# Linear attention and two layers: inputs that come transposed, keys' exponentials on ScalarE, another order, and half the numerators as float32 products

## The chip, the core and the metric

The kernel runs on one core of a Trainium2 chip. The metric is the time on the device, in microseconds (us), of one execution. The engines work through their own instruction streams in order and wait for each other by semaphores: PE multiplies matrices, DVE and ACT work on vectors, POOL does so too, SP issues the transfers. PE's results land in PSUM (eight banks); the other operands lie in SBUF.

## What is computed

Attention with 4 batches of 8 heads, 576 rows, head size 64 and 128 features, and then two layers over 2304 tokens (512 wide, 2048 inner). The weights of the layers come as float64.

```python
def phi(x):
    proj = np.einsum('bhsd,df->bhsf', x, w_phi)
    proj = proj - np.max(np.abs(proj), axis=-1, keepdims=True)
    return np.concatenate([np.exp(proj), np.exp(-proj)], axis=-1)
q_p, k_p = (phi(q), phi(k))
kv = np.einsum('bhsf,bhsd->bhfd', k_p, v)
z = np.sum(k_p, axis=2)
num = np.einsum('bhsf,bhfd->bhsd', q_p, kv)
den = np.einsum('bhsf,bhf->bhs', q_p, z)[..., None] + 1e-06
return (num / den).astype(np.float32)
```

The first layer is `g = h * (1 / (1 + exp(-h)))` with `h = x @ w_in`, the second `g = h * cos(h)`, each followed by `g @ w_out`.

## The kernel before

The 32 heads go in eight sets of four. A product of high accuracy is made of float32r parts: an operand is cast to float32r (hi), the rest is subtracted (lo), and three products hi·hi, hi·lo, lo·hi are added. Products of the keys with the values (kv) are plain float32.

For a set, `load_qk` brings queries and keys as rows; `transpose_in` (L270) turns them on PE into PSUM, ACT casts the result to hi (L284), DVE makes lo (L285). `phi` (L290) makes the projections of one unit (unit 0: the tails of four heads, units 1 to 4: 512 rows of one head each) in a PSUM bank `p`; DVE takes the largest absolute value (L304) and subtracts it (L306). For the keys, `k_exp` lets ACT write both exponentials (L315, L316). For the queries, `q_exp` transposes on PE into the bank `t2` (L324), ACT makes the exponentials (L332), POOL casts them to hi, `qh` (L338), and `q_rest` makes the lower parts `ql` (L346) on DVE or POOL. `kv_parts` sums keys times values (L360 for the tails, L363), cast by ACT (L367), with lo by DVE (L368). `num_parts` makes the numerators and a row of denominators: for each pair of heads (p = 0 or 1) four parts of six products of 288 columns (L389 to L391). `Norm.take` copies them out on ACT (L172); `invert` inverts the denominators on DVE and spreads them by way of two transfers (L186, L189); `apply` multiplies on POOL (L197, L200) into `xy`, the layers' input, which `Inputs.split` parts again (L473, L474).

The order is written by hand. `START` lists the pieces of the first set, `PERIOD` those of one period, in which the queries of a set meet the keys of the next; every piece issues its instructions on all engines at once, so that one list sets the order on each. A name as phi.k.2 is a step, its operand and its unit; a + is one set later, a - one earlier. `piece` is a quarter of the preparation of one weight chunk on ACT, DVE and POOL (L103 to L126). PSUM's banks in the attention: 2 for transposes, 2 for `p`, 1 for `t2`, 3 shared by kv and numerators.

The layers follow (`moe`): h by PE (L509), the functions by ACT, DVE and POOL, y by PE (L558 to L565).

Of the kernel before, what the change touches and what calls it, by code (L numbers as in the profile page):

```python
# [30 lines left out]

MAGIC = 12582912.0
# [16 lines left out]
START = parse("""  # L49
T.k.2 w load.v T.k.0 T.k.1 load.k+ phi.k.0 kx.0 phi.k.1 T.q.0 phi.k.2 phi.k.3 kx.1 T.q.2 kv.0.0.0 kx.2 phi.k.4 kx.3  # L50
kv.0.0.1 phi.q.0 T.k.2+ kx.4 kv.1.0.0 phi.q.1 qx.0 T.q.1 phi.q.2 T.k.0+ kv.1.0.1 qx.1 phi.q.3 ql.1.g T.k.1+ kv.0.1.0
qx.2 phi.q.4 load.k++ ql.2.v kv.1.1.0 qx.3 ql.0.g kv.0.1.1 load.q+ kv.1.1.1 qx.4
# [3 lines left out]
kx.1+ x.2+ num.1.1 x.3+ phi.k.2+ T.k.0++ phi.q.0+ num.1.0 x.4+ load.q++ kx.2+ num.1.2 x.5+ kv.0.0.0+ inv.0 phi.k.0++  # L56
T.k.1++ T.q.2++ num.1.3 x.6+ qx.0+ piece phi.q.1+ ql.0.g+ phi.q.2+ kv.1.0.0+ kv.0.0.1+ piece qx.1+ phi.q.4+ app.0
kv.0.1.0+ qx.2+ ql.1.v+ inv.1 phi.q.3+ kv.0.1.1+ piece qx.4+ kv.1.0.1+ ql.2.v+ kv.1.1.0+ qx.3+ phi.k.3++ T.q.1++
kv.1.1.1+ load.k+++ num.0.0+ kx.0++ ql.3.v+ phi.k.4++ num.0.1+ T.k.2+++ load.v++ num.0.2+ x.0++ kx.3++ kx.4++
phi.k.1++ ql.4.v+ app.1 num.0.3+ x.1++ T.q.0++ piece  # L60
# [3 lines left out]
class Weights:  # L64
    """float64 weights, given as raw words, to float32 parts hi + lo of 12 and 12 bits."""
# [68 lines left out]
class Queue:  # L134
    """Pieces of the weights' conversion, taken one after the other."""
# [23 lines left out]
class Norm:  # L159
    """Numerators over denominators, to x, [dm, token]."""  # L160
# [30 lines left out]
    def apply(self, n, p):  # L191
        nc, xy = self.nc, self.xy
# [7 lines left out]
        nc.gpsimd.tensor_mul(xy[rows, B * NJ + b // 2, c0:c0 + 2, at], t[rows, :, SM:S], r[rows, :, SM:S])  # L200


def attention(tc, q, k, v, w_phi, norm, pieces, then):
    nc = tc.nc
    W = D + 1
    with ExitStack() as ctx:
# [5 lines left out]
        kr, krt, qr, qrt = {}, {}, {}, {}  # L212

        def load_qk(n, src, main, tails, name):
            b, h0 = divmod(n, 2)
            h0 *= 4
            t = fp.tile([P, 4, NJ, D], F32, name=f"{name}r")
            u = fp.tile([P, 2, D], F32, name=f"{name}rt")
            for i in range(2):
                nc.sync.dma_start(u[64 * i:64 * i + 64], src[b, h0 + 2 * i:h0 + 2 * i + 2, SM:S, :].rearrange("h s d -> s h d"))  # L220
            nc.sync.dma_start(t, src[b, h0:h0 + 4, 0:SM, :].rearrange("h (p j) d -> p h j d", j=NJ))
            main[n], tails[n] = t, u
# [33 lines left out]
        # Stationary operands of the last product: columns 0..64 [kv | z] of even heads, 63..127 [z | kv] of odd ones.  # L256
        kvs = [[sp.tile([P, 2, 2, M], F32R, name=f"kv{i}_{part}") for part in ("hi", "lo")] for i, M in enumerate((W, P))]
# [10 lines left out]
        tT = {}  # L268

        def transpose_in(n, name, i):  # L270
            main, tails = (kr, krt) if name == "k" else (qr, qrt)
            N = SM if i < 2 else P
            ps = pp.tile([P, N], F32, name="tp", tag="tp", bufs=2)
            if i < 2:
                for c in range(4):
                    x, jj = divmod(c, 2)
                    src = main[n][:, i + 2 * x, 2 * jj:2 * jj + 2, :].rearrange("p j d -> p (j d)")
                    nc.tensor.transpose(ps[:, c * P:(c + 1) * P], src, ident)
            else:
                nc.tensor.transpose(ps, tails[n].rearrange("p a d -> p (a d)"), ident)  # L280
            sfx = "m" if i < 2 else "t"
            hi = fp.tile([P, N], F32R, name=f"{name}T_hi{sfx}", bufs=2 if i < 2 else 1)
            lo = fp.tile([P, N], F32R, name=f"{name}T_lo{sfx}", bufs=2 if i < 2 else 1)
            nc.scalar.copy(hi, ps)  # L284
            nc.vector.tensor_sub(lo, ps, hi.bitcast(F32))  # L285
            tT[n, name, i] = (hi, lo)
# [3 lines left out]
        def phi(n, name, u):  # L290
            """Unit 0: the tails of the four heads; 1 + 2 p + x: head p + 2 x."""
            i = 2 if u == 0 else (u - 1) // 2
            ns = 1 if u == 0 else 2
            hi, lo = tT[n, name, i]
            ps = pp.tile([P, ns, 2 * F], F32, name="p", tag="p", bufs=2)
            for s in range(ns):
                c = 0 if u == 0 else (((u - 1) % 2) * 2 + s) * P
# [13 lines left out]
        def k_exp(n, u):  # L311
            src = pm.pop((n, "k", u))
# [6 lines left out]
        def q_exp(n, u):  # L319
            src = pm.pop((n, "q", u))  # L320
            ns = 2 if u == 0 else 4
            ps = pp.tile([P, ns, P], F32, name="t2", tag="t2", bufs=1)
            for i in range(ns):
                nc.tensor.transpose(ps[:, i, :], src[:, i, :], ident)  # L324
            if u == 0:
                for p in range(2):
                    qh[n, p] = sp.tile([P, 2, 2, S], F32R, name=f"qh{p}")
                    ql[n, p] = sp.tile([P, 2, 2, S], F32R, name=f"ql{p}")
            p, x = divmod(u - 1, 2)
            for c in range(2):  # L330
                e = sp.tile([P, ns, P], F32, name="et" if u == 0 else "e", bufs=2 if u == 0 else 4)
                nc.scalar.activation(e, ps, AF.Exp, scale=1.0 - 2.0 * c)  # L332
                if u == 0:
                    parts = [(e[:, i, :].rearrange("p (x s) -> p x s", x=2), *(t[n, i][:, c, :, SM:S] for t in (qh, ql))) for i in range(2)]
                else:
                    parts = [(e.rearrange("p a s -> p (a s)"), *(t[n, p][:, c, x, 0:SM] for t in (qh, ql)))]
                for i, (ev, hi, lo) in enumerate(parts):
                    nc.gpsimd.tensor_scalar(hi, ev, 1.0, 0.0, op0=ALU.mult, op1=ALU.add)  # L338
                    rests[n, u, c, i] = (lo, ev, hi)

        def q_rest(n, u, engine):
            """The lower parts of the queries' exponentials."""
            for c in range(2):
                for i in range(2 if u == 0 else 1):
                    lo, ev, hi = rests.pop((n, u, c, i))
                    engine.tensor_sub(lo, ev, hi.bitcast(F32))  # L346
# [3 lines left out]
        def kv_parts(n, p):  # L350
            """18 products of heads p and p + 2: sums over rows of phi(k) with v and ones."""
            out = []

            def mm(c, i):
                def go():
                    if (n, p) not in kvp:
                        kvp[n, p] = pp.tile([P, 2, 2, W], F32, name="kv", tag="kn", bufs=3)
# [7 lines left out]
                    if (c, i) == (1, 8):  # L365
                        hi, lo = (t if p == 0 else t[:, :, :, D - 1:P] for t in kvs[p])
                        nc.scalar.copy(hi, ps)  # L367
                        nc.vector.tensor_sub(lo, ps, hi.bitcast(F32))  # L368
# [334 lines left out]
```

## Time and profile before

| what | us |
|---|---|
| three runs | 1050.23, 1051.86, 1052.01 (median 1051.86) |
| span of the profiled execution, first to last instruction | 1048.8 |
| attention, to the first product of the layers | 228.6 |
| the two layers | 820.2 |

The time of the profiled execution itself is its span of 1048.8 us and what lies around it; the runs shown are 1.4 to 3.2 us above that span. Busy shares of the whole span (PE 97%, DVE 68%, ACT 39%, POOL 35%) are averages over two stages with different limits, so the rows below are taken from the attention by itself.

### The profile page before, as it was taken

What the parts mean: (1) busy time and instruction counts of PE and PEld (TensorE: products, weight loads), DVE (VectorE), ACT (ScalarE), POOL (GpSimd) and SP (SyncE); (2) the same over time, 40 slices, a digit from 0 to 9 for tenths busy, and PEclk for the clock granted to TensorE, in tenths of its full rate; (3) what the DMA queues carried; (4) which work ended last, traced back from release to release, by engine and by line L of the source; (5) the groups of instructions that cost most, each with busy time, mean ns of one, the idle gap of its engine ahead of it and who ended that gap; (6) DMA issues with size and microseconds to landing.
All of it is one profiled execution on the core that took longest, in us unless ns stands there. A gap on an engine that the chain in (4) does not pass through costs nothing.

```text
span 1048.8 us, 15083 instructions
## 1 busy us (share of the span) xinstructions
PE 1019.1 (97%) x6000; PEld 972.5 (93%) x6000; DVE 711.9 (68%) x956; ACT 407.8 (39%) x664; POOL 369.4 (35%) x426
## 2 busy tenths in 40 slices
PE   7999999999999999999999999999999999999998
PEld 7989999989999999999999999899888988998997
DVE  6999999978544344544545567667677867786764
ACT  5655566544433222222223333444333333333332
POOL 3566666656122111201211024334434433343221
PEclk9999999999999999999999999999999999999999
DMA  4544333114111101110110111101110111100112
GB/s 118 139 112 112 99 105 81 47 40 129 41 41 46 55 22 61 41 41 21 61 48 34 41 41 42 40 21 61 41 41 21 61 40 41 27 34 1 61 57 63
DMA packets 62757, 58.33 MB, mean 56 GB/s; under 512 B 30560, under 2 KB 55264, under 8 KB 62688
## 3 DMA queue, kind: packets, MB, share of 16 engines
q1 hardware_dynamic: 62688, 57.38, 18.5%
q8 instruction: 47, 0.77, 0.3%
q14 instruction: 22, 0.18, 0.1%
HBM read 52.49 MB, written 4.79 MB: 55 GB/s over the span
## 4 chain that ended last, share of the span: by engine, by line
PE 61%; DVE 25%; POOL 7%; ACT 4%; issue 1%; DMA 1%; SPq 0%; POOLq 0%; ACTq 0%; DVEq 0%
PE h L509 24%; PE y L558 6%; PE y L560 6%; PE y L559 6%; DVE ql L346 4%; DVE tb L531 3%; DVE tb L530 3%; DVE tb L535 3%; PE kv L363 3%; POOL ta L529 2%; PE y L563 2%; PE y L564 2%; PE y L565 2%; DVE xy L589 2%; POOL gh L536 2%; DVE gl L538 2%
## 5 line engine op out<-in xcount | busy, mean ns | idle before, releaser
L509 PE MATMUL h<-xh,win_hi 128*128 128x384 f32 x768 | 259.1, 337 | 1.7 <-DVE tb L535 1.7
L509 PE MATMUL h<-xl,win_hi 128*128 128x384 f32 x768 | 258.8, 337 | 0.3 <-DVE xl L474 0.3
L509 PE MATMUL h<-xh,win_lo 128*128 128x384 f32 x768 | 258.7, 337 | 0.0
L521 DVE SCALAR_TENSOR_TENSOR ta<-ta,h 128x768 f32<-128x768 f32 x48 | 45.8, 953 | 177.7 <-ACT ta L520 177.7
L509 PEld LDWEIGHTS h<-xh,win_hi 128*128 128x128 f32 x768 | 144.2, 188 | 4.7 <-PE y L565 2.6
L509 PEld LDWEIGHTS h<-xl,win_hi 128*128 128x128 f32 x768 | 144.2, 188 | 2.4 <-DVE xl L474 0.6
L509 PEld LDWEIGHTS h<-xh,win_lo 128*128 128x128 f32 x768 | 144.2, 188 | 0.0
L532 ACT ACTIVATE tb<-tb 128x768 f32<-128x768 f32 x48 | 40.7, 847 | 239.0 <-DVE tb L531 239.0
L558 PE MATMUL y<-gh,wout_hi 128*128 128x384 f32 x384 | 129.5, 337 | 0.2 <-ACT xy L587 0.2
L560 PE MATMUL y<-gh,wout_lo 128*128 128x384 f32 x384 | 129.6, 337 | 0.0
L559 PE MATMUL y<-gl,wout_hi 128*128 128x384 f32 x384 | 129.4, 337 | 0.0
L520 ACT ACTIVATE ta<-h 128x768 f32<-128x768 f32 x48 | 39.0, 813 | 206.4 <-PE h L509 203.1
L563 PE MATMUL y<-wout_hi,gh 128*128 128x512 f32 x288 | 115.0, 399 | 3.3 <-ACT xy L587 1.8
L564 PE MATMUL y<-wout_lo,gh 128*128 128x512 f32 x288 | 114.4, 397 | 0.0
L565 PE MATMUL y<-wout_hi,gl 128*128 128x512 f32 x288 | 114.4, 397 | 0.0
L536 POOL TENSOR_SCALAR gh<-tb 128x768 fp32r<-128x768 f32 x48 | 46.9, 977 | 186.0 <-DVE tb L535 176.0
L538 DVE TENSOR_TENSOR gl<-tb,gh 128x768 fp32r<-128x768 f32 x48 | 75.4, 1570 | 34.3 <-POOL gh L536 34.3
L121 POOL TENSOR_SCALAR wout_hi<-wt 128x512 fp32r<-128x512 f32 x32 | 27.8, 869 | 200.3 <-DVE wt L118 171.1
L121 POOL TENSOR_SCALAR win_hi<-wt 128x512 fp32r<-128x512 f32 x32 | 21.6, 675 | 187.1 <-DVE wt L118 187.1
L589 DVE TENSOR_TENSOR xy<-y,xy 128x384 f32<-128x384 f32 (+1 forms) x126 | 70.8, 606 | 9.7 <-PE y L560 6.0
L535 DVE TENSOR_TENSOR tb<-tb,h 128x768 f32<-128x768 f32 x48 | 45.6, 951 | 46.7 <-ACT tb L533 46.2
L558 PEld LDWEIGHTS y<-gh,wout_hi 128*128 128x128 f32 x384 | 72.1, 188 | 0.5 <-ACT xy L587 0.5
(114 smaller groups left out, 2082.6 us busy)
## 6 DMA issues: line engine op xcount, KB each, us to landing
raw<-in_moe_w_in SPq DMA_DIRECT2D x32, 512.0 KB, 3.6
raw<-in_moe_w_out SPq DMA_DIRECT2D x32, 512.0 KB, 3.6
rb<-rd SPq DMA_DIRECT2D x16, 288.0 KB, 3.6
kr<-in_k SPq DMA_DIRECT2D x8, 512.0 KB, 4.3
qr<-in_q SPq DMA_DIRECT2D x8, 512.0 KB, 4.1
va<-in_v SPq DMA_DIRECT2D x32, 128.0 KB, 4.1
out<-xy SPq DMA_DIRECT2D x16, 256.0 KB, 2.2
krt<-in_k SPq DMA_DIRECT2D x16, 32.0 KB, 3.1
```

The costliest lines, as they stand in the source:

```text
L121: nc.gpsimd.tensor_scalar(hi, t.bitcast(F32), 1.0, 0.0, op0=ALU.mult, op1=ALU.add)
L509: nc.tensor.matmul(o, a[:, cs], x[t][:, :, c, :], start=first, stop=(c == NC - 1 and a is lo))
L535: nc.vector.tensor_mul(b, b, h)
L536: nc.gpsimd.tensor_scalar(hi, b, 1.0, 0.0, op0=ALU.mult, op1=ALU.add)
L538: nc.vector.tensor_sub(lo, b, hi.bitcast(F32))
L558: nc.tensor.matmul(o, wh[:, ds], hi[:, f, :], stop=False, **st)
L559: nc.tensor.matmul(o, wh[:, ds], lo[:, f, :], start=False, stop=False)
L560: nc.tensor.matmul(o, wl[:, ds], hi[:, f, :], start=False, stop=en)
L563: nc.tensor.matmul(o, hi[:, f, ds], wh, stop=False, **st)
L564: nc.tensor.matmul(o, hi[:, f, ds], wl, start=False, stop=False)
L565: nc.tensor.matmul(o, lo[:, f, ds], wh, start=False, stop=en)
L589: nc.vector.tensor_tensor(y, o, y, op=ALU.add)
```

## The change

Queries and keys arrive transposed: the host lays out each set as 128 partitions by 1152 columns (the tails in the first 128), one load each. `transpose_in` and its bank are gone; `split_in` (piece sp) casts to hi on the named engine (A: ACT, D: DVE, G: POOL) and subtracts on DVE from SBUF. The values are loaded in another order of rows, and the tokens of a block now follow each other in the output.

With engine A, `phi` negates the maximum on POOL. For the keys nothing is subtracted any more: ACT reads the bank `p` and applies the maximum as a bias, in slices of 128 columns. The banks are now 3 for `p`, 2 for `t2`, 3 for kv and numerators.

For the heads with p = 1 (`FULL`), ACT writes the queries' exponentials straight to `qh` in float32, there is no `ql`, kv is copied in float32, and a numerator is two float32 products instead of six. `apply` runs on DVE for all but the last set. START and PERIOD are new; all numerators of a set now stand at the start of the next period, and app.1 goes to the start of the one after.

```diff
+PB, T2, KN = 3, 2, 3
+FULL = (1,)
...
 PERIOD = parse("""
-kx.1+ x.2+ num.1.1 x.3+ phi.k.2+ T.k.0++ phi.q.0+ num.1.0 x.4+ load.q++ kx.2+ num.1.2 x.5+ kv.0.0.0+ inv.0 phi.k.0++
...
+app.1.D- num.0.0 x.6+ num.0.1 phi.k.2.A+ kx.1+ load.v+ num.0.2 num.0.3 kx.2+ x.0+ phi.q.1.D+ piece sp.k.0.G++
...
-            nc.gpsimd.tensor_mul(xy[rows, b * NJ:(b + 1) * NJ, c0 + x, :], t[rows, x, 0:SM].rearrange("p (j n) -> p j n", n=P),
+            engine.tensor_mul(xy[rows, b * NJ:(b + 1) * NJ, c0 + x, :], t[rows, x, 0:SM].rearrange("p (j n) -> p j n", n=P),
...
+        def split_in(n, name, i, engine):
+            at = slice(0, P + SM) if i == 0 else slice(P + SM, GC)
+            hi, lo = xT[n, name, i] = [fp.tile([P, at.stop - at.start], F32R, name=f"{name}T_{part}{i}") for part in ("hi", "lo")]
+            src = raw[n, name][:, at]
+            cast(engine, hi, src)
+            nc.vector.tensor_sub(lo, src, hi.bitcast(F32))
...
+            if engine == "A":
+                nm = sp.tile([P, 2 * ns], F32, name="nm", bufs=3)
+                nc.gpsimd.tensor_scalar(nm, m, -1.0, 0.0, op0=ALU.mult, op1=ALU.add)
+                if name == "k":
+                    pm[n, name, u] = pv, m, nm
+                    return
...
-            nc.scalar.activation(t[:, 0], src, AF.Exp)
-            nc.scalar.activation(t[:, 1], src, AF.Exp, scale=-1.0)
+            for i in range(ns if m is not None else 0):
+                nc.scalar.activation(t[:, 0, i], src[:, i], AF.Exp, bias=nm[:, i:i + 1])
+                nc.scalar.activation(t[:, 1, i], src[:, i], AF.Exp, bias=m[:, i:i + 1], scale=-1.0)
...
+            for i in full:
+                for c in range(2):
+                    src = ps[:, i, :].rearrange("p (x s) -> p x s", x=2) if u == 0 else ps.rearrange("p a s -> p (a s)")
+                    nc.scalar.activation(qh[n, i][:, c, :, SM:S] if u == 0 else qh[n, i][:, c, x, 0:SM], src, AF.Exp, scale=1.0 - 2.0 * c)
...
+                        if p in FULL:
+                            nc.tensor.matmul(o, kvs[p][0][:, c, x, :], qh[n, p][:, c, x, at], start=(c == 0), stop=(c == 1))
+                            continue
```

How instructions move on three engines (names as above; the numbers in them only tell buffers apart):

DVE, before, in the middle of a period: the last unit of queries, two lower parts, an inverse.

```order
L304 TENSOR_REDUCE m<-p 128x4
L306 TENSOR_TENSOR pm<-p,m 128x512
L346 TENSOR_TENSOR ql_1102<-e,qh_1101 128x512 x2
L183 TENSOR_SCALAR r<-den 128x9
L184 RECIPROCAL r<-r 128x9
```

DVE, after, where one period passes into the next.

```order
L397 TENSOR_TENSOR kv_lo<-kv,kv_hi 128x260
L307 TENSOR_REDUCE m<-p 128x2
L307 TENSOR_REDUCE m<-p 128x4
L374 TENSOR_TENSOR ql_625<-e,qh_624 128x512 x2
L280 CAST qT_hi_792<-qr 128x640
L290 TENSOR_TENSOR qT_lo_793<-qr,qT_hi_792 128x640
L205 TENSOR_TENSOR xy<-xn_542,rb 64x4x128 x2
L208 TENSOR_TENSOR xy<-xn_542,rb 64x2x64
```

The pair of lower parts remains once in a period on DVE; the reductions of keys stand without a subtraction, and the split of the inputs and the multiplications of app have come to DVE.

POOL, before, the second half of its period.

```order
L338 TENSOR_SCALAR qh_1101<-e 128x512 x2
L121 TENSOR_SCALAR win_hi<-wt 128x512
L338 TENSOR_SCALAR qh_1103<-e 128x512 x4
L197 TENSOR_TENSOR xy<-xn_998,rb 64x4x128 x2
L200 TENSOR_TENSOR xy<-xn_998,rb 64x2x64
L126 TENSOR_TENSOR win_lo<-wt,win_hi 128x512
```

POOL, after, from the cast of the next keys to the negations of the next units 0 and 1.

```order
L129 TENSOR_SCALAR win_hi<-wt 128x512
L310 TENSOR_SCALAR nm<-m 128x4
L282 TENSOR_SCALAR qh_977<-et 128x2x64 x2
L282 TENSOR_SCALAR qh_977<-e 128x512 x2
L374 TENSOR_TENSOR ql_978<-e,qh_977 128x512 x2
L374 TENSOR_TENSOR ql_978<-et,qh_977 128x2x64 x2
L134 TENSOR_TENSOR win_lo<-wt,win_hi 128x512
L310 TENSOR_SCALAR nm<-m 128x2
```

The multiplications and most casts have left; lower parts of the queries and the negations, which the keys' exponentials wait for, have come.

PE, before, a part of the numerators of p = 1 and the unit after it.

```order
L389 MATMUL num<-qh_302,kv_hi 128x288
L390 MATMUL num<-ql_303,kv_hi 128x288
L391 MATMUL num<-qh_302,kv_lo 128x288
L299 MATMUL p<-wphi,kT_him 128x256
L300 MATMUL p<-wplo,kT_him 128x256
L301 MATMUL p<-wphi,kT_lom 128x256
```

PE, after, the last part of p = 1 and what follows it.

```order
L417 MATMUL num<-qh_626,kv_all 128x288 x2
L388 MATMUL kv<-vt_105,kpt 128x130
L391 MATMUL kv<-va,kp 128x65 x4
L341 MATMUL t_974<-ident,pmt 128x128 x2
L341 MATMUL t_988<-ident,pm 128x128 x4
```

A part of p = 1 is two products where it was six, and no transposes of inputs stand between.

## Rows read from the trace of the kernel before

**Rows 1.** Windows by stage: stretch, its us, busy (instructions), granted clock, DMA share, GB/s.

```profile
0.00:29.93 29.93, 23.81 (x185) 23.35 (x186) 21.16 (x40) 16.57 (x33) 11.51 (x37) 1.00 0.49 136
29.93:221.40 191.47, 177.50 (x1451) 174.94 (x1449) 182.82 (x293) 112.82 (x253) 119.26 (x166) 0.97 0.36 93
221.40:228.62 7.22, 7.22 (x50) 7.13 (x50) 6.53 (x8) 4.56 (x13) 4.61 (x5) 0.87 0.04 9
228.62:1048.80 820.18, 810.60 (x4322) 767.04 (x4320) 501.38 (x618) 273.89 (x368) 234.01 (x220) 1.00 0.14 44
```

**Rows 2.** Windows: sum and mean of four periods, 43.88 to 156.23.

```profile
sum 112.35, PE 104.18 PEld 102.86 DVE 108.18 ACT 66.07 POOL 71.54; mean PE 26.05 PEld 25.71 DVE 27.04 ACT 16.52 POOL 17.89
```

**Rows 3.** DVE by line, those four periods: form, count, busy us, mean ns, idle.

```profile
L346 DVE TENSOR_TENSOR ql<-e,qh 128x512 fp32r<-128x512 f32 x32 | 37.5, 1212 | 0.0
L306 DVE TENSOR_TENSOR pm<-p,m 128x512 f32<-128x512 f32 x33 | 22.8, 691 | 1.1
...
L285 DVE TENSOR_TENSOR kT_lom<-tp,kT_him 128x512 fp32r<-128x512 f32 x8 | 5.5, 682 | 0.2 <-ACT kT_him L284 0.2
L285 DVE TENSOR_TENSOR qT_lom<-tp,qT_him 128x512 fp32r<-128x512 f32 x8 | 5.4, 679 | 0.0
...
L368 DVE TENSOR_TENSOR kv_lo<-kv,kv_hi 128x260 fp32r<-128x260 f32 x8 | 3.4, 420 | 0.3 <-ACT kv_hi L367 0.3
...
L285 DVE TENSOR_TENSOR qT_lot<-tp,qT_hit 128x128 fp32r<-128x128 f32 x4 | 1.1, 280 | 0.0
```

**Rows 4.** One line's instructions, whole run: ns min/median/max, first and last start, form.

```profile
L346 DVE TENSOR_TENSOR ql<-e,qh x62: 677/922/2987, 26.4 to 226.5; 128x512 fp32r<-128x512 f32 x62
```

```profile
L285 DVE TENSOR_TENSOR qT_lom<-tp,qT_him x16: 675/678/692, 12.0 to 204.2; 128x512 fp32r<-128x512 f32 x16
```

```profile
L107 DVE TENSOR_SCALAR wt<-raw x64: 415/420/1353, 42.6 to 955.6; 128x512 int32<-128x512 int32 x64
```

**Rows 5.** Timeline of PE in one period: start us, us, line, form, count.

```profile
120.06 0.30 PE L391 MATMUL num<-qh,kv_lo 128*128 128x288 f32 x1
120.20 0.28 PE L299 MATMUL p<-wphi,kT_him 128*128 128x256 f32 x1
120.31 0.28 PE L300 MATMUL p<-wplo,kT_him 128*128 128x256 f32 x1
...
128.04 0.39 PE L360 MATMUL kv<-vt,kpt 128*128 128x130 f32 x2
128.26 1.90 PE L363 MATMUL kv<-va,kp 128*128 128x65 f32 x16
130.00 0.61 PE L324 MATMUL t<-ident,pm 128*128 128x128 f32 x4
```

**Rows 6.** Timeline of PE at a gap: in brackets the idle time and its releaser.

```profile
110.23 0.70 PE L324 MATMUL t<-ident,pm 128*128 128x128 f32 x4 [1.87 <-DVE pm L306]
```

**Rows 7.** ACT by line in the four periods.

```profile
L315 ACT ACTIVATE kp<-pm 128x512 f32<-128x512 f32 x16 | 10.1, 634 | 3.4 <-DVE pm L306 3.3
...
L284 ACT CAST kT_him<-tp 128x512 fp32r<-128x512 f32 x8 | 4.7, 591 | 1.0 <-PE tp L278 1.0
...
L332 ACT ACTIVATE et<-t 128x256 f32<-128x256 f32 x8 | 2.7, 391 | 0.0
...
L284 ACT CAST kT_hit<-tp 128x128 fp32r<-128x128 f32 x4 | 1.1, 265 | 0.0
```

**Rows 8.** POOL by line in the four periods.

```profile
L197 POOL TENSOR_TENSOR xy<-xn,rb 64x512 f32<-64x512 f32 x16 | 23.2, 1471 | 0.3
L338 POOL TENSOR_SCALAR qh<-e 128x512 fp32r<-128x512 f32 x32 | 22.6, 727 | 4.7 <-ACT e L332 4.7
```

**Rows 9.** Transfers by line: KB each, median us from issue to landing.

```profile
rb<-rd SPq DMA_DIRECT2D x16, 288.0 KB, 3.6
```

**Rows 10.** Timeline of PE: the first product of features, and the layers' start.

```profile
8.18 0.56 PE L299 MATMUL p<-wphi,kT_hit 128*128 128x256 f32 x1
...
229.26 0.44 PE L509 MATMUL h<-xl,win_hi 128*128 128x384 f32 x1 [0.30 <-DVE xl L474]
```

More of the change, by code (lines that the diff above doesn't have):

```diff
@@ L30 @@
 GF = FF // P // NG
+GC = P + 4 * 2 * P
+PB, T2, KN = 3, 2, 3
+FULL = (1,)
 MAGIC = 12582912.0
@@ L189, in invert, with apply @@
         nc.sync.dma_start(self.rb[n][64 * p:64 * p + 64].rearrange("p x s -> p (x s)"), d.to_broadcast([64, 2 * S]))
-    def apply(self, n, p):
-        nc, xy = self.nc, self.xy
+    def apply(self, n, p, engine):
+        xy = self.xy
         b, c0 = n // 2, (n % 2) * 2
@@ L196, in apply @@
         for x in range(2):
-            nc.gpsimd.tensor_mul(xy[rows, b * NJ:(b + 1) * NJ, c0 + x, :], t[rows, x, 0:SM].rearrange("p (j n) -> p j n", n=P),
+            engine.tensor_mul(xy[rows, b * NJ:(b + 1) * NJ, c0 + x, :], t[rows, x, 0:SM].rearrange("p (j n) -> p j n", n=P),
                                  r[rows, x, 0:SM].rearrange("p (j n) -> p j n", n=P))
         at = slice(64 * (b % 2), 64 * (b % 2) + 64)
-        nc.gpsimd.tensor_mul(xy[rows, B * NJ + b // 2, c0:c0 + 2, at], t[rows, :, SM:S], r[rows, :, SM:S])
+        engine.tensor_mul(xy[rows, B * NJ + b // 2, c0:c0 + 2, at], t[rows, :, SM:S], r[rows, :, SM:S])
 def attention(tc, q, k, v, w_phi, norm, pieces, then):
@@ L210, in attention, with load_qk @@
         pp = ctx.enter_context(tc.tile_pool(name="at_ps", bufs=1, space=PSUM))
[L212 to L222, printed above, removed]
+        raw = {}
+        def load_qk(n, src, name):
+            t = fp.tile([P, GC], F32, name=f"{name}r")
+            nc.sync.dma_start(t, src[n])
+            raw[n, name] = t
         def load_v(n):
@@ L255, in attention @@
                 nc.gpsimd.memset(t[64 * x:64 * x + 64, i % 2, c:c + 1], 1.0)
-        kvs = [[sp.tile([P, 2, 2, M], F32R, name=f"kv{i}_{part}") for part in ("hi", "lo")] for i, M in enumerate((W, P))]
+        kvs = [[sp.tile([P, 2, 2, M], F32 if i in FULL else F32R, name=f"kv{i}_{part}") for part in (("all",) if i in FULL else ("hi", "lo"))]
+               for i, M in enumerate((W, P))]
         for t in kvs[1]:
@@ L266, in split_w @@
             nc.vector.tensor_sub(wplo, wff, wphi.bitcast(F32))
[L268 to L278, printed above, removed]
-            else:
[L280 to L286, printed above, removed]
+        xT = {}
@@ new lines, in attention, with cast @@
+        engines = {"D": nc.vector, "A": nc.scalar, "G": nc.gpsimd}
+        def cast(engine, out, src):
+            if engine == "A":
+                nc.scalar.copy(out, src)
+            elif engine == "D":
+                nc.vector.tensor_copy(out, src)
+            else:
+                nc.gpsimd.tensor_scalar(out, src, 1.0, 0.0, op0=ALU.mult, op1=ALU.add)
+        def split_in(n, name, i, engine):
[4 more added lines that the diff above has]
+            nc.vector.tensor_sub(lo, src, hi.bitcast(F32))
@@ L326, in q_exp @@
                 for p in range(2):
-                    qh[n, p] = sp.tile([P, 2, 2, S], F32R, name=f"qh{p}")
-                    ql[n, p] = sp.tile([P, 2, 2, S], F32R, name=f"ql{p}")
+                    qh[n, p] = sp.tile([P, 2, 2, S], F32 if p in FULL else F32R, name=f"qh{p}")
+                    if p not in FULL:
+                        ql[n, p] = sp.tile([P, 2, 2, S], F32R, name=f"ql{p}")
             p, x = divmod(u - 1, 2)
-            for c in range(2):
-                e = sp.tile([P, ns, P], F32, name="et" if u == 0 else "e", bufs=2 if u == 0 else 4)
-                nc.scalar.activation(e, ps, AF.Exp, scale=1.0 - 2.0 * c)
+            full = [i for i in range(2) if i in FULL] if u == 0 else [p] if p in FULL else []
@@ new lines, in q_exp @@
+            for i in full:
+                for c in range(2):
+                    src = ps[:, i, :].rearrange("p (x s) -> p x s", x=2) if u == 0 else ps.rearrange("p a s -> p (a s)")
+                    nc.scalar.activation(qh[n, i][:, c, :, SM:S] if u == 0 else qh[n, i][:, c, x, 0:SM], src, AF.Exp, scale=1.0 - 2.0 * c)
+            parts = rests[n, u] = []
+            if u and full or len(full) == 2:
+                return
+            es = [sp.tile([P, ns, P], F32, name="et" if u == 0 else "e", bufs=2 if u == 0 else 4) for _ in range(2)]
@@ L333, in q_exp @@
+            for c, e in enumerate(es):
                 if u == 0:
-                    parts = [(e[:, i, :].rearrange("p (x s) -> p x s", x=2), *(t[n, i][:, c, :, SM:S] for t in (qh, ql))) for i in range(2)]
-                else:
[L336 to L339, printed above, removed]
+                    for i in range(2):
+                        if i not in full:
+                            parts += [(c, e[:, i, :].rearrange("p (x s) -> p x s", x=2), *(t[n, i][:, c, :, SM:S] for t in (qh, ql)))]
+                    at = slice(1 if 0 in full else 0, 1 if 1 in full else 2)
+                else:
+                    parts += [(c, e.rearrange("p a s -> p (a s)"), *(t[n, p][:, c, x, 0:SM] for t in (qh, ql)))]
+                    at = slice(0, ns)
+                nc.scalar.activation(e[:, at], ps[:, at], AF.Exp, scale=1.0 - 2.0 * c)
+                for c2, ev, hi, _ in parts:
+                    if c2 == c:
+                        cast(engine, hi, ev)
@@ L341, in q_rest @@
         def q_rest(n, u, engine):
[L343 to L346, printed above, removed]
+            for _, ev, hi, lo in rests.pop((n, u)):
+                engine.tensor_sub(lo, ev, hi.bitcast(F32))
         kvp = {}
@@ L365, in go @@
                     if (c, i) == (1, 8):
-                        hi, lo = (t if p == 0 else t[:, :, :, D - 1:P] for t in kvs[p])
+                        hi, *lo = (t if p == 0 else t[:, :, :, D - 1:P] for t in kvs[p])
                         nc.scalar.copy(hi, ps)
-                        nc.vector.tensor_sub(lo, ps, hi.bitcast(F32))
+                        if lo:
+                            nc.vector.tensor_sub(lo[0], ps, hi.bitcast(F32))
                 return go
@@ L402, in step @@
                 return then(front)
-            key = (n, name, *arg)[:3] if name == "ql" else (n, name, *arg)
+            key = (n, name, *(a for a in arg if a not in engines))
             if key in done or not 0 <= n < NQ:
@@ L570, in store @@
             if b < B:
-                nc.sync.dma_start(out[b * S:b * S + SM, :].rearrange("(p j) n -> p j n", j=NJ)[:, j, :], y)
+                nc.sync.dma_start(out[b * S + j * P:b * S + (j + 1) * P, :], y)
             else:
@@ L692 @@
     for name in ("q", "k", "v", "w_phi", "moe_w_in", "moe_w_out", "moe2_w_in", "moe2_w_out"):
-        a = np.ascontiguousarray(inputs[name])
+        a = inputs[name]
+        if name in ("q", "k"):
+            x = np.asarray(a).reshape(2 * B, 4, S, D)
+            main = x[:, [0, 2, 1, 3], :SM].reshape(2 * B, 4, 2, 2, P, D).transpose(0, 3, 5, 1, 2, 4).reshape(2 * B, P, 8 * P)
+            tail = x[:, :, SM:].reshape(2 * B, 2, 2, S - SM, D).transpose(0, 2, 4, 1, 3).reshape(2 * B, P, P)
+            a = np.concatenate([tail, main], axis=2)
+        a = np.ascontiguousarray(a)
         if a.dtype == np.float64:
```

70 lines of the change are left out of this document (39 added, 31 removed).

## Prediction

> **What bounds the kernel now.** I read the busy times by stage first [rows 1]. From 228.62 us on, in the two layers, PE is busy 810.6 of 820.2 us, and no instruction there changes: that stretch stays. So all is decided in the 228.6 us of the attention. From the first numerators of the first four heads (29.93) to those of the last four (221.40) run seven periods in 191.47 us, 27.35 each; 7.2 us of last numerators follow.
>
> Then the means of four whole periods [rows 2]: of 28.09 us DVE is busy 27.04, PE 26.05, POOL 17.89, ACT 16.52. PE's records overlap, so I count PE by the distance of their starts [rows 5]: 0.131 us for a product of the numerators (288 columns), 0.119 for one of the features, 0.109 for a record at L363 (16 in 1.74), 0.11 at L360 and for a transpose. A period has 48, 54, 64, 8 and 36 of them: 6.3 + 6.4 + 7.0 + 0.9 + 4.0 = 24.6 us. DVE is thus the bound, and PE waits for it: 1.87 us before the transposes of a unit [rows 6]. The stretch's granted clock of 0.97 [rows 1] is what such gaps leave of 2.4 GHz; some of it ran at 1.2.
>
> DVE's largest item is the lower parts of the queries' exponentials: L346, 37.5 us in four periods, 9.4 in each [rows 3]. Alone it takes 677 ns, at worst 2987, while L285, of the same size but with one input in PSUM, always takes 675 to 692 [rows 4]. So an instruction of DVE with both inputs in SBUF pays for POOL's work beside it, and DVE's load depends on POOL's.
>
> **The change part by part, for one period.**
>
> PE. The 18 transposes of the inputs go: -2.0. Of the numerators 24 products go (-3.14) and 8 float32 products come. A float32 product leaves two records: where the program has one product of L360 and eight of L363, the profile has 2 and 16 [rows 5]. So 16 records of 288 columns, a form that the trace does not show. The upper bound is L360's pace, 130 columns in 0.11, that is 0.85 ns a column and 0.244 for 288; the lower is 0.131, the pace of the products that go, since 65 columns take 0.109 too and the load of the stationary may set both [rows 5]. I take 0.244, the only float32 row with more columns: 3.9, net +0.8 (lower bound: 2.1, net -1.0). PE comes to 24.6 - 2.0 + 0.8 = 23.4, at least 21.6.
>
> The Trainium skill (FP8 and Floating Point Precision, TensorE Precision Notes) says that true float32 takes four passes through the array. Worked out from that, 4 x 288 columns at 2.4 GHz are 0.48 us a product, an estimate; PE would come to 23.4 by it, and the lower bound would fall. No run here shows it.
>
> DVE. What goes: the lower parts from PSUM (8 x 0.68 + 8 x 0.68 + tails of 0.28, 3.3 a period), half of the subtractions L306 (those of the keys, 4 x 0.69 and a small one, 3.2), one of two kv_lo (0.4), six of eight ql of 512 columns at their mean of 1.21 (7.3): -14.2 [rows 3]. What comes: four lower parts of the inputs, now with both inputs in SBUF (2304 columns, 4.5 times 512): 3.05 at 677 ns, 5.45 at 1212; three casts (1664 columns): 1.4 at L107's 420 ns, 2.2 at 677 [rows 4]; the multiplications of app that POOL gives up (4 of 512 columns, 2 of 128): 3.3 to 5.4. Together +7.75 to +13.05. If the two ql that stay ran alone, 1.1 more would go. So DVE comes to 19.5 (nothing of POOL beside it) or to 25.9 (as much as now). POOL loses four L197 (5.8), six casts (4.4) and some small ones, and gets two ql, a cast of 640 columns and five tiny negations (about 4): some 10 of 24 us instead of 17.9 of 28.1 [rows 2, 8]. At that share, six tenths, DVE stands at 23.4; as POOL's long instructions now lie mostly beside DVE's reads of PSUM, I take 23.
>
> ACT. The keys' exponentials become 36 slices of 128 columns, with a bias each. Nearest rows: 265 ns for 128 columns without one, 391 for 256 [rows 7]; 9.5 to 14.1. What goes: 8 exponentials of 0.63 and two small ones (5.9), four casts of 0.59 and two of 0.27 (2.9); two casts of the queries come (1.2), and 0.3 for the tails. 16.5 - 8.8 + 1.5 + 9.5 to 14.1 = 18.7 to 23.3. Under PE in either case: no term.
>
> A new wait. A bank of the features' product is now held through reduction, negation on POOL and eight slices on ACT; the next product that wants it waits on PE, and all of PE behind it. There are three banks instead of two. Adding up PE's order, unit 4 of the keys ends 9.4 us into a period, its slices stand on ACT behind two units of the queries and end near 15.5, and the product that wants the bank comes at 17.8. So 0, with 2 us in hand.
>
> Transfers. SP issues one load for each of keys and queries instead of three. They are issued some 13 us into a period and wanted after 23; a landing like the broadcast's takes 3.6 [rows 9]. So 0. The inverses and the two transfers behind them end near 16 where DVE wants them for app at 16.2. It used to be POOL that waited; now up to 1 us of DVE, under PE: 0.
>
> Start and end. The features begin at 8.18 [rows 10], behind transposes and two rounds of casts; the keys' load is now the first issue, and a cast and a subtraction remain. Following each engine's order with the rows' durations I get the first numerators at 27.7 instead of 29.93: -2.2 (0 to -4). At the end eight parts of numerators follow each other, 4 x 0.79 + 4 x 0.98 = 7.1, and the last split of the layer's inputs comes after them, where PE waited 0.30 [rows 10] and may now wait 1: 8.1.
>
> **The sum.** PE at 23.4, DVE at 23. The engine that bounds now has 1.05 us of waits in a period (28.09 - 27.04); I keep 1.0: 24.4. The last period lacks two units of keys (9 x 0.119): 23.4. 27.7 + 6 x 24.4 + 23.4 + 8.1 = 205.6, against 228.6: -23.0. The profiled span of 1048.8 becomes 1025.8. The runs shown end 1.4 to 3.2 us above that span; from the median, 1051.86 - 23.0 = 1028.9. For the period I allow 23.6 to 25.5: 1023 to 1037.
>
> **Rivals.**
>
> A. A float32 record keeps to 0.131. PE needs 21.6, DVE bounds with 22.5: a period of 23.3, 1021. For it: 65 and 130 columns have one pace [rows 5]. Against it: nothing says that the load still covers 288.
>
> B. DVE stays the bound. Its new instructions all have both inputs in SBUF, and cost 1212 ns and not 677 for 512 columns. With 25.9 and 1.0 of waits the period is 26.9: -5.5, 1046. For it: L346's spread [rows 4]. Against it: POOL loses its longest item, L197 [rows 8].
> The Trainium skill (SBUF — State Buffer, Who interferes with whom) states this as a rule: DVE with two SBUF inputs shuts out, or is shut out by, a GpSimd instruction that reads SBUF, for the whole instruction, and so do casts that use both ports; this speaks against moving splits and app to SBUF inputs on DVE. Rows 4 agree for the subtractions; no row shows the casts.
>
> C. Slower: POOL's queue holds up the keys. The negations stand in order behind the queries' casts, two ql and a weight's lower part: two casts of 0.73 and two lower parts priced as L197's 1.47 [rows 8], and about 3 us of smaller ones, some 7.5 us of work from about 12.4 into a period to 20, when the next keys' negation is due at 20.8. If that work takes 1.6 times as long beside DVE, it ends near 24.5 and the first slices come 3.8 us late, ACT's copy of kv and the last exponentials stand behind them, and PE's numerators behind these: 28.2 a period, 1055. It decides from a delay of 3.3 us (a period of 27.7 is today's time). For it: L338 and L197 vary with DVE. Against it: 1.6 is more than their means show.
>
> **How the numbers follow.** Forecast 66%, A 12%, B 13%, C 9%. The predicted time is the forecast's, 1029. Low 1019 takes in A; high 1044 takes in the forecast and the milder half of B. Within 0.2% (2 us, about what these runs can tell from no change) falls only a narrow strip between B and C, 4%; slower 9%; faster 87%.
>
> **What would show it.** Right: periods near 24.4 us between the first numerators of successive heads, first ones near 27.7, PE busy without gaps over 1 us, two records of 0.24 at the new product, DVE near 23, the layers at 820. Wrong: splits and app on DVE above 1 us for 512 columns (B); negations that start long after their reductions and PE waiting for a bank (C); a record at 0.13 (A); any change of the layers.

## The result, and the profile after

The changed kernel takes 1020.77 us (median of 4, 1020.54 to 1020.96), the kernel before in the same session 1051.05: a ratio of 0.9725, 95% interval 0.9704 to 0.9747. The forecast was 1029.0, with a range of 1019 to 1044. The profiled span fell from 1048.8 to 1018.8 us.

Lines moved: the features' products are now L302 to L304, their maximum L307, the subtraction L319, the transposes L341, the keys' slices L332 and L333, the lower parts of the queries L374, those of the inputs L290, app L205 and L208, the numerators in parts L421 to L423, and the float32 product L417. Rows below also name the casts L278 (ACT) and L280 (DVE), the negation of a maximum L310 (POOL), the lower part of kv L397, the copies of numerators L180 and the first step of an inverse L191.

Windows of the changed kernel by stage, as [rows 1]: us, then busy time (instructions) of PE, PEld, DVE, ACT and POOL, granted clock, DMA share, GB/s.

```profile
0.00:27.98 27.98, 20.92 (x153) 19.59 (x154) 18.34 (x34) 18.03 (x57) 8.10 (x35) 1.00 0.52 149
27.98:191.79 163.81, 162.70 (x1280) 156.35 (x1280) 145.26 (x258) 133.17 (x426) 69.60 (x109) 1.00 0.41 108
191.79:199.69 7.90, 7.35 (x43) 6.16 (x41) 2.75 (x7) 5.63 (x14) 0.14 (x2) 1.00 0.04 4
199.69:1018.80 819.11, 808.92 (x4320) 766.01 (x4320) 501.87 (x617) 273.32 (x367) 233.06 (x218) 1.00 0.14 44
```

Four whole periods, as [rows 2]:

```profile
sum 93.62, PE 93.62 PEld 90.02 DVE 86.05 ACT 76.63 POOL 42.40; mean PE 23.41 PEld 22.51 DVE 21.51 ACT 19.16 POOL 10.60
```

93.62 us for four periods are 23.40 each, and PE is busy in all of it: no PE wait is listed in that stretch. DVE needs 21.51, ACT 19.16, POOL 10.60. The only wait of PE in all seven periods is one of 1.1 us in the sixth, where before it waited up to 1.9 us in each [rows 6]. The waits of the seven periods (us in total, times, longest), first in the changed kernel, then in the kernel before:

```profile
PE t L341 <- DVE pm L319: 1.1, 1, 1.1
```

```profile
PE t L324 <- DVE pm L306: 12.7, 7, 1.9
```

One thing more differs. In the kernel before, three periods at a granted clock of 1.00 took 26.5 to 26.8 us, and three at 0.92 to 0.96 took 28.1 to 29.1; one of each:

```profile
85.55:114.25 28.70, 26.83 (x213) 26.67 (x212) 27.54 (x45) 16.54 (x38) 18.31 (x26) 0.92 0.40 106
142.33:168.88 26.55, 24.68 (x212) 24.57 (x212) 25.67 (x43) 15.44 (x35) 16.63 (x23) 1.00 0.34 86
```

DVE is the busiest engine in both, so the bound was read rightly, but the three periods at the lower clock are together some 6 us longer than the other three, out of the 27.7 us that the seven periods lost. No run separates the clock from the work.

PE's timeline at the numerators of two odd heads, as [rows 5]; a float32 product is two records:

```profile
102.67 0.28 PE L304 MATMUL p<-wphi,qT_lo 128*128 128x256 f32 x1
102.79 2.10 PE L417 MATMUL num<-qh,kv_all 128*128 128x288 f32 x8
104.51 0.50 PE L302 MATMUL p<-wphi,kT_hi 128*128 128x256 f32 x1
104.84 0.29 PE L303 MATMUL p<-wplo,kT_hi 128*128 128x256 f32 x1
...
107.49 1.14 PE L417 MATMUL num<-qh,kv_all 128*128 128x288 f32 x4
108.46 0.39 PE L388 MATMUL kv<-vt,kpt 128*128 128x130 f32 x2
```

Four records take 108.46 - 107.49 = 0.97 us, 0.243 each. For the eight, L302's own start is drawn early (its next product follows after 0.33 and not 0.12); from 102.79 to 104.84 less one product of 0.12 are 1.93, again 0.24 each.

DVE by line in the four periods, as [rows 3]: form, count, busy us, mean ns.

```profile
L205 DVE TENSOR_TENSOR xy<-xn,rb 64x512 f32<-64x512 f32 x16 | 11.4, 749 | 0.1
...
L208 DVE TENSOR_TENSOR xy<-xn,rb 64x128 f32<-64x128 f32 x8 | 6.6, 821 | 0.0
L290 DVE TENSOR_TENSOR qT_lo<-qr,qT_hi 128x640 fp32r<-128x640 f32 (+1 forms) x8 | 6.1, 759 | 0.3
L290 DVE TENSOR_TENSOR kT_lo<-kr,kT_hi 128x640 fp32r<-128x640 f32 (+1 forms) x8 | 6.0, 756 | 0.1
L374 DVE TENSOR_TENSOR ql<-e,qh 128x512 fp32r<-128x512 f32 x9 | 5.8, 684 | 0.0
```

The lower parts of the queries, 1212 ns in [rows 3], take 684; 757 for the mean of 640 and 512 columns is the same price per column. It is mainly app that still shares time with POOL: its small multiplications take 0.29 us at the least and 0.82 in the mean, its large ones 0.68 and 0.75.

Waits in the four periods (engine and line, what it waited for: us in total, times, longest):

```profile
POOL nm L310 <- DVE m L307: 23.4, 13, 3.1
POOL nm L310 <- ACT kp L333: 16.9, 4, 4.2
ACT kpt L332 <- POOL nm L310: 11.5, 4, 2.9
```

The keys' negations on POOL wait for their reductions. Where the row names ACT it is no other: in the period from 98.13 us each starts within 0.2 us of the end of its reduction, so the one put down to ACT at 102.55 follows a reduction that ends at 102.39. ACT waits 2.9 us a period for one of them, but ACT has 4.2 us free in a period and nothing on PE waits for it.

### The profile page after: what moved, and what is told of

Its sections match the earlier page's. It is cut to its first block, busy times and chain, and to the rows that moved or that the text cites. A ratio compares the mean times of both kernels' runs of the same rounds, so it can differ in the third digit from the quotient of the medians.

```text
span 1018.8 us, 14733 instructions
## 1 busy us (share of the span) xinstructions
PE 999.9 (98%) x5792; PEld 948.1 (93%) x5792; DVE 668.2 (66%) x913; ACT 430.2 (42%) x861; POOL 310.9 (31%) x363
## 4 chain that ended last, share of the span: by engine, by line
PE 79%; DVE 11%; POOL 5%; ACT 3%; issue 1%; DMA 1%; SPq 0%; POOLq 0%; ACTq 0%; DVEq 0%
PE h L541 31%; PE y L590 7%; PE y L592 7%; PE y L591 7%; PE kv L391 5%; PE y L595 4%; PE y L596 4%; PE y L597 4%; PE num L417 3%; DVE tb L563 2%; DVE tb L562 2%; DVE tb L567 2%; PE p L302 2%; PE p L304 2%; POOL ta L561 2%; PE p L303 2%
## 5 line engine op out<-in xcount | busy, mean ns | idle before, releaser
L592 PEld LDWEIGHTS y<-gh,wout_lo 128*128 128x128 f32 x384 | 72.1, 188 | 0.0
```

What stands on the lines that cost most here:

```text
L592: nc.tensor.matmul(o, wl[:, ds], hi[:, f, :], start=False, stop=en)
```

## The experiments

All are edits of the changed kernel, so a difference is against its 1020.8 us (the kernel before, run beside each, had medians of 1048.9 to 1051.1, so 1 to 2 us of a difference mean little); the period is the mean distance of the first numerators of successive fours of heads, 23.4 us in it.

### What holds the period

**More work on PE.** Each transpose of the queries' units is issued twice.

```diff
-            for i in range(ns):
+            for i in (*range(ns), *range(ns)):
                 nc.tensor.transpose(ps[:, i, :], src[:, i, :], ident)
```

> The changed kernel with each transpose of a unit of the queries issued twice into the same bank: 18 more transposes a period on PE, and nothing else. At 0.11 us a transpose record, two records each, that is 4.0 us, or 2.0 us if the second record overlaps as rows 5 count them for 36 records of a period (36 x 0.11 for 18 transposes); I price 18 more transposes as 18 x 0.11 = 2.0 us. Theory: PE alone sets the period, since it is busy 23.41 of 23.41 us there, so the period rises one for one to 25.4 and the time by 7 x 2.0 = 14 us and up to 2 us at the start: 1035 to 1037. Rival: PE's busy time hides waits inside its records, which the added work would fill; then DVE with 21.5 us is as near to the bound, and the rise is less than 7 us.

Measured: 1034.74 us (ratio to the kernel before 0.9863, 0.9849 to 0.9878), 14.0 us more. Windows of four of its periods:

```profile
54.95:156.09 101.14, 101.14 (x811) 97.76 (x809) 86.92 (x153) 78.31 (x244) 42.67 (x64) 1.00 0.40 111
```

25.29 a period, 1.89 more, and PE again busy throughout: 18 transposes at 0.105 us went into the time one for one. PE sets the period, and its busy time hides no waits. (The sentence ahead of the price in the expectation names 4.0 us; the price used, 2.0, is the one that held.)

**Less work on PE.** The second of each part's two float32 products is left out.

```diff
-    nc.tensor.matmul(o, kvs[p][0][:, c, x, :], qh[n, p][:, c, x, at], start=(c == 0), stop=(c == 1))
+    if c == 0:
+        nc.tensor.matmul(o, kvs[p][0][:, c, x, :], qh[n, p][:, c, x, at], start=True, stop=True)
```

> The changed kernel without the second of the two float32 products of each part (the numerators of the odd heads are incomplete): 8 records of 0.244 us fewer in a period, so PE needs 23.4 - 1.95 = 21.45 us, just under DVE's 21.5. Theory: PE was the bound, so the period falls until DVE holds it. If a period held by DVE carries 1.0 us of waits as the kernel before did, it is 22.5; if it carries none, 21.6. With 1 us less at the end: 1020.8 - 6.3 - 1.0 = 1013.5, or 1020.8 - 12.6 - 1.0 = 1007. Rival: DVE was already the bound, or both are through a loop between engines: no more than 2 us faster.

Measured: 1017.5 us (0.970, 0.9676 to 0.9723), only 3.3 us less. Windows of four periods, and then all waits of PE in them (us in total, times, longest):

```profile
50.70:144.01 93.31, 88.06 (x707) 84.74 (x705) 84.53 (x153) 76.35 (x245) 43.14 (x65) 1.00 0.42 120
```

```profile
PE t L341 <- DVE pmt L319: 3.6, 4, 0.9
PE t L341 <- DVE pm L319: 1.3, 1, 1.3
```

Undisturbed periods are 23.02. Neither the theory (1007 or 1013.5) nor the rival (no more than 2 us faster) held. With less of its own work PE waits again for DVE before the queries' transposes, as it did before the change, though DVE is busy only 21.1 us: a chain through DVE stands 0.4 us behind PE. My 21.6 to 22.5 was too low; this chain has 1.9 us of DVE's waits in it, not 1.0.

**More work on DVE.** Two or four copies of a spare tile in each app.

```diff
+        if n < NQ - 1:
+            for _ in range(2):      # 4 in the other run
+                engine.tensor_copy(self.spare, self.spare)
         at = slice(64 * (b % 2), 64 * (b % 2) + 64)
```

> The changed kernel with two copies of a spare tile (512 float32 columns, SBUF to SBUF, nobody waits for them) on DVE in each of the two app of a period: at the 0.42 to 0.49 us of L280's casts, 1.7 to 2.0 us a period. DVE is busy 21.5 of 23.4 us. Theory (a loop of DVE, PE and ACT stands at 23.0, as the run without half of the float32 products showed: 21.1 us of DVE and 1.9 of its waits): only 0.4 us are free, so the period is 24.7 to 25.0 and the time 1020.8 + 9 to 11 = 1030 to 1032. Rival (DVE's idle time is slack): the 1.9 us swallow it, 1020 to 1023.

> As the run before it, with four copies in each app: 3.4 to 3.9 us of DVE more in a period. Theory (loop at 23.0): 26.4 to 26.9, the time 1020.8 + 21 to 25 = 1042 to 1046. Rival (idle time is slack): DVE at 24.9 to 25.4 sets the period without waits, 1020.8 + 10 to 14 = 1031 to 1035. Whichever holds, two more copies must cost their full price over the run with two.

Measured: 1025.27 us (0.976, 0.9734 to 0.9787) and 1035.03 (0.9855, 0.9834 to 0.9875), that is 4.5 and 14.3 us more. A copy takes 427 ns (median), so 1.7 and 3.4 us of DVE's time were added to a period of which 0.64 and 2.04 show (a seventh of the 4.5 and 14.3). With two copies neither range held; with four the time stands at the upper edge of the rival's 1031 to 1035, but the two further copies cost 1.4 us a period and not their full 1.7. So 1.0 to 1.4 of DVE's 1.9 us of idle time can be used, and the rest stays idle. With two copies four periods in seven are within 0.2 us of the changed kernel's or below; the others are longer by 0.6 to 3.4.

**All numerators as float32 products.**

```diff
-FULL = (1,)
+FULL = (0, 1)
```

> The changed kernel with the numerators of all four heads as float32 products (FULL holds both pairs): 24 records of 0.131 us go, 16 of 0.244 come, so PE needs 0.77 us more in a period, 24.2. DVE loses the last six lower parts of the queries and of kv (about 4 us, to 17.5), ACT two casts, POOL two lower parts and four casts. Theory (PE alone sets the period; a float32 product costs two records by its columns): 7 x 0.77 = 5.4 us more and 0.8 at the end, 1027. Rival (the other engines' waits hold part of the 23.4): their relief outweighs PE's load, 1021 or less.

Measured: 1028.48 us (0.9789, 0.9766 to 0.9813), 7.7 us more. Windows of four periods:

```profile
52.72:151.27 98.55, 96.61 (x706) 86.50 (x705) 77.25 (x141) 73.10 (x237) 15.71 (x32) 1.00 0.41 114
```

```profile
PE t L341 <- DVE r L191: 1.5, 3, 0.5
PE t L341 <- DVE pm L319: 0.5, 1, 0.5
```

24.64 a period: PE is busy 24.15, 0.75 more, which is the price of the products (16 at 0.243 for 24 at 0.131), and 0.49 are a wait for DVE that stands once in each period before a transpose. Relief of DVE (19.3) and POOL (3.9) buys nothing. So the price of a float32 product is confirmed, but PE alone doesn't set this period; why that order leaves 0.49 us was not followed up.

### What keeps PE from waiting

**Banks.** First the features' and the transposes' banks as before the change, then only the features'.

```diff
-PB, T2, KN = 3, 2, 3
+PB, T2, KN = 2, 1, 3        # the second run: 2, 2, 3
```

> The changed kernel with the PSUM banks of the kernel before for the features' products and the queries' transposes: two and one in place of three and two (two banks stay empty). No work changes. Theory: PE runs without a wait because its next product finds a free bank while DVE, POOL and ACT still read the others; with fewer the keys' eight slices (2 us and more on ACT behind the negation) hold a bank that PE wants, waits come back, and the period is 24.4 or more: 1028 and above. Rival: the order of the work alone removes the waits, PE's queue is never short of a bank: within 2 us of the changed kernel.

> The changed kernel with two banks for the features' products instead of three, and still two for the queries' transposes. With both cut the period was 28.8 us, 5.4 above the changed kernel's; of PE's waits listed there some four fifths stood at the features' first product, behind DVE's subtractions and the keys' slices. Theory (the features' banks are what feeds PE): the period is 27 to 28, that is 1046 to 1053. Rival (the single bank of the transposes made the loss, and the waits at the features followed from it): the period stays below 24.5, that is below 1029.

Measured: 1068.75 us (1.0178, 1.0134 to 1.0221) and 1054.33 (1.004, 1.0022 to 1.0057): slower than the kernel before by 1.8% and 0.4%, with periods of 28.8 and 27.5 us and no work added. Where PE stands with two banks for the features, all its waits in four periods and one of them in its timeline:

```profile
PE p L302 <- DVE pmt L319: 8.4, 4, 2.1
PE p L302 <- DVE r L191: 2.2, 4, 0.5
PE p L302 <- DVE pm L319: 1.2, 4, 0.3
PE p L302 <- ACT kp L333: 1.0, 4, 0.2
```

```profile
98.68 0.28 PE L304 MATMUL p<-wphi,qT_lo 128*128 128x256 f32 x1
101.04 0.36 PE L302 MATMUL p<-wphi,kT_hi 128*128 128x256 f32 x1 [2.08 <-DVE pmt L319]
```

Every wait is at the first product of a unit, for a bank that is still being read. The row that names the inverse (r L191) stands for the subtraction before it: in the period from 89.63 us that subtraction ends at 106.85 and PE goes on 0.15 us later, as it does behind the two other subtractions. So 11.8 of the 12.8 us are waits for the queries' subtractions on DVE, the longest for that of the tails, which stands behind the preparation of weights in DVE's order; the keys' slices, which the first expectation blamed, are named for 1.0.

The third bank decides the sign of the change in this order, which was made for three: with two it is 33.6 us slower, some 29 in the seven periods and 5 in the start (first numerators at 33.07 us instead of 27.98). A part of that is the clock, 0.98 in these periods. A third bank in the order of the kernel before was not tried.

### What each part of the change is worth

**The keys' maxima subtracted on DVE again** (phi.k.0 to phi.k.4 with D in place of A in the tables).

> The changed kernel with the maxima of the keys subtracted on DVE again (phi.k with D in place of A): the 36 slices with a bias become 8 exponentials of 0.63 us and two small ones on ACT, DVE gets four subtractions of 0.69 us and a small one, POOL loses five negations. DVE then needs 21.5 + 3.0 = 24.5 us in a period, ACT about 16, PE still 23.4. Theory: DVE becomes the bound, and the period is 24.5 without waits to 25.5 with 1.0 us of them: 1020.8 + 7.7 to 14.7 = 1028.5 to 1035.5. Rival: the slices of the keys on ACT, at 19.2 us with waits for POOL, held the period as much as PE did; then the time stays within 3 us of the changed kernel.

Measured: 1036.37 us (0.9879, 0.9864 to 0.9895), 15.6 more. Windows of four periods:

```profile
80.07:183.41 103.34, 94.89 (x740) 90.53 (x738) 99.77 (x173) 60.23 (x141) 39.96 (x44) 1.00 0.37 98
```

25.83 a period, of which DVE is busy 24.94: it is the bound, and 0.9 us of idle time on it are back, as in the kernel before (1.05). Both stand a little above the forecast of 24.5 to 25.5 and 1028.5 to 1035.5.

**app on POOL again** (app.0 and app.1 with G in place of D).

> The changed kernel with the multiplications by the inverses (app) on POOL again, as in the kernel before: DVE loses 3.3 us a period (21.5 to 18.2), POOL gains about 6 us (10.6 to 17), and app.0 stands right in front of the negations of the next keys on POOL's queue. Theory (PE alone sets the period, with 2 us and more in hand at the negations): no change, 1019 to 1023. Rival C of the prediction: the longer queue of POOL makes the negations late by about 4 us and more, the features' banks stay taken, and the period grows by 1 us or more: 1028 and above. Rival: DVE held the period in part: 2 to 5 us faster.

Measured: 1020.44 us (0.9728, 0.9713 to 0.9742): no change. Windows of four periods:

```profile
51.62:145.22 93.60, 93.60 (x739) 90.00 (x738) 74.48 (x129) 76.46 (x246) 67.23 (x89) 1.00 0.45 120
```

DVE is busy 18.6 us a period, POOL 16.8, PE all of 23.4. DVE saves 2.9 us, though app took 4.5 there. The negations behind that longer queue do no harm. The contention that the prediction feared is there, though: the same lower part in the changed kernel, in this one, and POOL beside it in this one.

```profile
75.91 0.83 DVE L290 TENSOR_TENSOR qT_lo<-qr,qT_hi 128x640 fp32r<-128x640 f32 x1
```

```profile
75.41 1.79 DVE L290 TENSOR_TENSOR qT_lo<-qr,qT_hi 128x640 fp32r<-128x640 f32 x1
```

```profile
75.11 3.24 POOL L205 TENSOR_TENSOR xy<-xn,rb 64x512 f32<-64x512 f32 x2
```

The rule of the Trainium skill (SBUF — State Buffer, Who interferes with whom) on DVE with two SBUF inputs against GpSimd agrees with these rows.

**All numerators in three products of parts, app on POOL**, and then the same with the last lower part issued a period's end earlier. Against the run just shown, the first of these differs in FULL = () alone, with two lower parts added to the start (ql.3, ql.4).

> A possible better version: the changed kernel with all numerators as three products of parts again, the lower parts of the odd heads' queries on DVE, their casts on ACT, and app on POOL. PE needs 23.4 - 0.8 = 22.6 us a period (24 records of 0.131 in place of 16 of 0.244), DVE 18.6 + 4 x 0.68 + 0.4 = 21.7, ACT 19.2 + 2.4 = 21.6, POOL about 17. If PE sets the period: 1020.8 - 7 x 0.8 - 0.4 = 1014.8. If the loop at 23.0 found above is one of DVE's order, which this moves little: 23.0 to 23.6, that is 1018 to 1022. If the float32 products are worth their place, since ACT and DVE are now both within 1 us of PE: above 1022.

```diff
-num.1.0 num.1.1 phi.k.3.A+ piece ql.4.D piece num.1.2
+num.1.0 num.1.1 phi.k.3.A+ piece piece num.1.2
-qx.4.A+ x.2+ sp.q.0.D++
+qx.4.A+ x.2+ ql.4.D+ sp.q.0.D++
```

> The run with all numerators in parts and app on POOL, with one more edit: the lower parts of the last odd unit of the queries (ql.4) move from between the odd heads' numerators to the end of the period before, so that PE no longer stands at num for ql, where it waited about 1.9 us a period. Theory 1 (the order, made for float32 numerators, puts that lower part too late, and this is what the parts cost): the period falls by 1.9 us from 27.5 to about 25.6, the time from 1053.6 to 1040. Theory 2 (the loss is the chain of ACT, DVE and PE that parts need at each step, casts, kv_lo and lower parts, and DVE's 23.3 us with its waits): what PE no longer waits there it waits at the next transposes or numerators, 1050 to 1056.

Measured: 1053.62 us (1.0038, 1.0026 to 1.0051) and 1052.78 (1.0039, 1.0021 to 1.0057). PE has 0.8 us less to do in a period, and the kernel is 33 us slower than with float32 numerators and app on POOL. PE's waits in four periods of the first, then of the second:

```profile
PE num L422 <- DVE ql L374: 7.8, 4, 2.0
PE num L421 <- ACT xn L180: 4.5, 4, 1.1
PE num L421 <- DVE kv_lo L397: 2.8, 4, 0.8
```

```profile
PE num L421 <- ACT xn L180: 4.5, 4, 1.1
PE num L421 <- DVE kv_lo L397: 2.7, 4, 0.7
PE p L302 <- DVE qT_hi L280: 2.6, 4, 0.7
PE t L341 <- ACT qh L278: 2.5, 4, 0.6
PE p L304 <- DVE qT_lo L290: 1.3, 4, 0.4
```

The wait for ql goes, and others come in its place, as theory 2 had it; the period falls only from 27.5 to 27.2. So, as far as these two orders show, the float32 numerators' gain is not PE's time, which they raise, but the casts and lower parts they spare ACT and DVE, and the waits of PE for these. An order made for parts throughout was not tried beyond this one move, so 33 us is what they are worth in this order, not in the best one.

Two parts of the change have no run of their own: the transposed inputs, whose 18 transposes a period would cost some 1.9 us on PE if they cost what those of the queries did above, and the new order itself.

## Why the prediction was right, and where it was off

| stage | before | predicted | measured |
|---|---|---|---|
| to the first numerators | 29.93 | 27.7 | 27.98 |
| seven periods | 191.47 | 169.8 | 163.81 |
| last numerators | 7.22 | 8.1 | 7.90 |
| layers | 820.18 | 820.2 | 819.11 |
| span | 1048.8 | 1025.8 | 1018.8 |

- **The bound and its size: right.** PE was put at 23.4 us a period, and the period is 23.40. The upper bound taken for a float32 record, 0.244, measures 0.243. The run with more transposes shows that PE sets the time, the run with all numerators in float32 confirms the price. The estimate worked out from the Trainium skill (FP8 and Floating Point Precision, TensorE Precision Notes), four passes, 0.48 us a product, agrees with 2 x 0.243.
- **The step that failed: "I keep 1.0: 24.4".** It carried 1.05 us of waits from a period that DVE held into one that PE holds. The forecast has 7.0 us of them in seven periods, the trace has one wait of 1.1; that is 5.9 of the 7 us by which the span was missed. The waits were those of the bound engine DVE, which stands in the middle of the chain and depends on others' results. They come back where DVE is made the bound again (0.9 with the keys' subtraction), and when PE's load is cut (PE waits for DVE, 23.02 a period). With PE as the bound and a third bank there are next to none in the changed kernel, with more transposes and with app on POOL; all numerators in float32 have 0.49, so a bound on PE doesn't remove them by itself.
- **DVE at 23: too high by 1.5, without effect.** Six tenths of the possible contention were assumed; the lower parts run at 684 and 757 ns, nearly alone. POOL's long instructions are not beside them in this order. Where app goes back to POOL and stands beside one of them, that lower part takes 1.79 us.
- **ACT and POOL: right in size.** 19.2 us (18.7 to 23.3 predicted) and 10.6 (some 10). For ACT with some luck: the slices' mean duration, 0.41 us, lies above the 0.391 of the upper bound, and what they cost, 36 at one start every 0.25 us or 9.0, lies below the 9.5 of the lower one.
- **The new wait for a features' bank, priced at 0: right,** and more rests on it than the text said: with two banks the period is 4.1 us longer and the change a loss. Chiefly the queries' subtractions hold the bank then, not the keys' slices that the prediction followed.
- **Start, tail: right** to 0.3 us. **Layers:** 1.07 us shorter, with no edit there; that was not explained.
- **The clock:** the prediction took 0.97 for what PE's gaps leave. That is too simple: with the keys' subtraction on DVE, PE waits 2.1 us a period at a granted clock of 1.00. The return to 1.00 had no term of its own in the sum.
- **Rival A** gave 1021, almost the measured time, but by a wrong way: its record of 0.131 and its bound on DVE are refuted. A time that fits a rival's number does not confirm it. **Rival B** falls with DVE's rows, and its chain is nonetheless near: 0.4 us behind PE. **Rival C** falls: in the changed kernel the negations stand behind their reductions, not behind POOL's queue, and with 6 us more on POOL's queue nothing changes.

No run beat the changed kernel by more than its spread with the whole of the work: app on POOL gives 1020.44. Since DVE's chain stands at 23.0 us, taking work from PE alone can bring at most 0.4 us a period, some 3 us.

## What to carry to other kernels

Here the waits found beside a bound went with that bound: when a change moves the bound to another engine, price them anew from that engine's own waits and from the buffers ahead of it, and don't carry them over. An operation may cost the bound engine more than what it replaces and still win, when it shortens the chain of others that feed it; and a bank that only lets the producer run ahead can decide the sign of the whole change.

## What the runs showed of the hardware

- A float32 product went by its columns between 130 and 288: about 0.11 us a record for 130 [rows 5], 0.243 for 288, both 0.84 to 0.85 ns a column. With 65 columns a record cost 0.109, as much as with 130; what sets the pace there was not tested.
- ACT's slices of 128 columns take 0.37 us but start every 0.25; a mean duration overstates what they cost.

Timeline of ACT at the keys' last unit in the changed kernel:

```profile
97.65 0.36 ACT L333 ACTIVATE kpt<-p,m 128x128 f32<-128x128 f32 x1
97.91 0.37 ACT L332 ACTIVATE kpt<-p,nm 128x128 f32<-128x128 f32 x1
98.16 0.38 ACT L333 ACTIVATE kpt<-p,m 128x128 f32<-128x128 f32 x1
```

- The granted clock was 1.00 wherever PE had no waits. With waits it was 0.97 in the kernel before [rows 1], 0.98 and 0.97 with two features' banks and with fewer of both, but still 1.00 with the keys' subtraction on DVE. With two features' banks PE was busy 1.90 of 4.00 us, and then the clock stood at 0.59, so for most of 4 us at 1.2 GHz:

```profile
126.00:130.00 4.00, 1.90 (x13) 1.58 (x12) 2.69 (x7) 2.57 (x9) 1.12 (x2) 0.98 0.02 1
130.00:134.00 4.00, 4.00 (x22) 3.76 (x21) 2.21 (x5) 1.06 (x6) 0.20 (x1) 0.59 0.51 141
```

In such a stretch of the kernel before, behind the gap of [rows 6], a features' product took 0.21 us instead of 0.119:

```profile
111.16 0.41 PE L301 MATMUL p<-wphi,kT_lom 128*128 128x256 f32 x1
111.37 0.41 PE L299 MATMUL p<-wphi,kT_him 128*128 128x256 f32 x1
```
